# Order of the first score tiles, transposes and squares, and the length of the first run of product halves, in a fused attention and maxout kernel

## The chip, the cores and the metric

The kernel runs on one core of one Trainium2 chip. The metric is device time in microseconds (us) of one execution; lower is better. A profiled execution gives, besides its time, its span from the first to the last instruction.

## The reference

Eight sequences of 3072 tokens go through a gated attention unit without softmax and then through a maxout layer with two input projections.

```python
# u, v: (8, 3072, 256); z: (8, 3072, 64); w1, w2: (256, 1024); w_out: (1024, 256)
scores = (1.0 / S) * np.matmul(z, z.transpose(0, 2, 1))
attn = np.maximum(scores, 0.0) ** 2
out = np.matmul(attn, v)
x = (u * out).reshape(B * S, D)
g = np.maximum(x @ w1, x @ w2)
return g @ w_out
```

## The kernel before

A sequence has 24 blocks of 128 tokens. A step is one window of 512 query tokens (4 blocks), so that there are 6 steps a sequence and 48 in all. Within a step the scores are made in tiles of two key blocks against 512 queries: four matmuls over 64 rows (`score`) write one PSUM pair of 128 x 1024. A relu reads it into SBUF as bf16, on ScalarE or VectorE, and a square follows in place, again on ScalarE or VectorE. The squared tiles multiply v into two accumulators in PSUM. Tiles are named by step and first key block: `("score", 0, 4)` is the third tile of the first step.

Score pairs live in three PSUM slots with the tags w0, w1 and w2 (the pool "mm"). A new tile in a slot waits for the reads of the slot's previous tile. The slots of the first four tiles are fixed as 1, 2, 1, 2; from the fifth tile on, `share_mm` takes for each the slot with the smallest `free_at`, the lower number on a tie.

The first three steps are "plain". In step 0 most products are done as halves: each matmul covers 64 rows of a key block, and the two halves go to the two accumulators. In mode A the first half goes to accumulator 0 and the second to accumulator 1, in mode B the other way round, so each block needs both an A and a B pass. `FIRST_RUNS` lists the runs of step 0 as (mode, first tile, end tile); `put_halves` puts each tile's four A or B matmuls per pair of blocks into the list of work. Between two runs a window of two score tiles is laid in (tiles 8 and 10 after the first run, 12 and 14 after the second, and so on). Where the mode changes, a mark (a nop on GpSimd's queue that waits for TensorE) keeps the two passes apart.

Before that stands the head, which is written out by hand at the end of the function. z is needed transposed (`zT`). The first nine blocks of z of the first sequence come by one DMA, are cast by VectorE and ScalarE, transposed on TensorE and copied to `zT` by VectorE (blocks 0 to 4) and ScalarE (5 to 8). The other blocks come by a second DMA; sixteen transposes write them to `tpz_c`, which takes the tag w0, and VectorE copies them in two parts of eight blocks. `head_pair(k0, part)` issues one part of one score tile of step 0: part 0 the scores, part 1 the relu (VectorE for tile 2, ScalarE for the others), part 2 the square (ScalarE for tile 0, VectorE for the others). The order of these calls is the order on each engine's queue:

```python
    head_pair(0, 0)
    head_pair(2, 0)
    head_pair(0, 1)
    head_pair(2, 1)
    ...  # tpz_c and its sixteen transposes
    head_pair(0, 2)
    ...  # VectorE's two copies
    head_pair(4, 0)
    head_pair(6, 0)
    head_pair(4, 1)
    head_pair(2, 2)
```

Everything else is ordered by a planner inside the kernel's Python. The order of TensorE's work (`pe_order`) follows from the list of work. For the other engines `find_orders` runs a greedy list schedule over assumed durations, which chooses the engine of each relu and square and the order on ScalarE, VectorE, SP (transposing DMAs and stores) and GpSimd's queue (loads). It is run 24 times with changed margins and the order with the earliest end is emitted. The jobs of the head are not planned: they count as done at the time that `HEAD_DONE` gives in nanoseconds, or else as done from the beginning. Wide SBUF tiles get their slots from a first pass of the same schedule (`share_wide`).

Of the kernel before, what the change touches and what calls it, by code (L numbers as in the profile page):

```python
# [11 lines left out]
def kernel(  # L12
# [23 lines left out]
    B, S, D = u.shape  # L36
# [87 lines left out]
    def zT_pe(zT, z_sb, s0, n, tpz=None):  # L124
        flat = z_sb.rearrange("p t d -> p (t d)")
        if tpz is None:
            tpz = mm_psum.tile([P, 8, P], bf16, name="tpz", tag="w0")
        for j in range(n):
            pin(nc.tensor.transpose(tpz[:, j, :], flat[:, ds((s0 + j) * dqk, P)], ident))  # L129
        return lambda copy: pin(copy(zT[:, ds(s0, n), :], tpz[:, :n, :]))  # L130
# [136 lines left out]
    def score(q, out_ps, j, k, s, q0, n):  # L267
        half = ds(j * dqk, dqk)
        matmul(
            out_ps,  # L270
            q.zT[half, k + 1 - j, :],
            q.zT[half, ds(G * s + 1 - j + q0, n), :],
            start=True,
            stop=True,
        )
# [4 lines left out]
    def relu(eng, out_ap, in_ap):  # L280
        if eng == "ACT":
            pin(nc.scalar.activation(out_ap, in_ap, AF.Relu))  # L282
        else:
            pin(nc.vector.tensor_single_scalar(out=out_ap, in_=in_ap, scalar=0.0, op=ALU.max))

    def square(eng, ap):
        if eng == "ACT":
            pin(nc.scalar.activation(ap, ap, AF.Square))  # L288
        else:
            pin(nc.vector.tensor_mul(ap, ap, ap))  # L290
# [21 lines left out]
    def a_tile(st, g):  # L312
        return tile_of(*a_key(st.n, g))
# [3 lines left out]
    def a_half(tile, k0):  # L317
        return tile[:, ds(k0 % G, 2), :].rearrange("p k x -> p (k x)")

    def a_rows(st, k0):  # L320
        return a_half(a_tile(st, k0 // G), k0).rearrange("p (t m x) -> p m t x", t=2, m=2)
# [94 lines left out]
    def s_tile(key):  # L416
        return tile_of("mm", key)

    def by_tokens(s_ps):
        return s_ps.rearrange("p m (t x) -> p m t x", t=2)  # L420
# [910 lines left out]

    turned_order = []
    plain_todo, plain_modes, first_windows = [], {}, []
    FIRST_RUNS = [("A", 0, 1), ("B", 0, 3), ("A", 1, 5), ("B", 3, 6), ("A", 5, 10), ("B", 6, 10)]

    for n, st in enumerate(steps):
        if not st.plain:
# [79 lines left out]
        if n == 0:  # L1417
            for run in FIRST_RUNS:
                first_windows.append(len(work))
# [335 lines left out]
    for pool in ("acc0", "acc1"):  # L1755
# [16 lines left out]
        A=NA, T=NT, es=6, lf=6, xT=LAG, g=2, o=2, e0=1, gs=1, xs=1, u=2, uT=2, mm=1000, acc0=1, acc1=1  # L1772
# [17 lines left out]
    for key, before in zip(pe_order, [None] + pe_order):  # L1790
        if key[0] == "score" and (before is None or plain_modes.get(before) == "F"):
            jobs[key].ways = {"PE": jobs[key].ways["PE"] + 2 * SWITCH}
    HEAD_DONE = {("relu", 0, 4): 900, ("square", 0, 2): 1400}
    HEAD_JOBS = HEAD | {("relu", 0, k0) for k0 in (0, 2, 4)} | {("square", 0, k0) for k0 in (0, 2)}


# [60 lines left out]
    def find_orders():  # L1857
# [14 lines left out]
        def settle(j, begin, ns):  # L1872
            j.begin, j.done = begin, begin + ns + j.lag
            if j.key in FIRST_LOADS:
                j.done = FIRST_LOADS[j.key]
            elif j.dma:

                dma_free[0] = max(dma_free[0], begin + DMA_START["SP" if "SP" in j.ways else "POOL"]) + (DMA_FULL if begin < DMA_FULL_TO else DMA_PART) * j.dma
                j.done = dma_free[0] + (DMA_LATE if begin > 125000 and j.key[0] != "zT" else DMA_END)
                if "SP" in j.ways:  # L1880
                    idle_from["SP"] = max(begin + SP_ISSUE, dma_free[0] - DMA_AHEAD)
            for nxt, _ in j.succ:
                nxt.waits -= 1
                if not nxt.waits:
                    release(nxt)
# [4 lines left out]
        for key in [k for k in jobs if k in HEAD_JOBS]:  # L1890
            settle(jobs[key], HEAD_DONE.get(key, -1), 0)
            for e in jobs[key].ways:
# [59 lines left out]
    def share_mm():  # L1952
        keys = order["mm"]
        uses = [[], [("mm", keys[0]), ("mm", keys[2])], [("mm", keys[1]), ("mm", keys[3])]]
        free_at, last_use = [0, 0, 1], [-1] * 3
        for key, slot in zip(keys, (1, 2, 1, 2)):
            bufs["mm", key].slot = slot
        for key in keys[4:]:
            at = position[taker["mm", key].key]
            slot = min([i for i in range(3) if last_use[i] < at], key=lambda i: free_at[i])  # L1960
            last_use[slot] = max(position.get(j.key, -1) for j in bufs["mm", key].jobs)
            user = pe_order[last_use[slot]]
            reads = 1200
            if key[0] == "o":
                reads = READ_O[0] if steps[key[1]].seven else READ_PLAIN[key[2] % 2]
            free_at[slot] = plan[user] + jobs[user].ways["PE"] + reads
            uses[slot].append(("mm", key))
            bufs["mm", key].slot = slot
        return uses
# [5 lines left out]
    find_orders()  # L1975
    wide = share_wide()
    pairs = share_mm()
    for _ in range(ROUNDS):
        link(wide + pairs)
# [15 lines left out]
    def take(pool, key):  # L1995
        b = bufs[pool, key]
        b.tile = b.make() if b.slot is None else b.make(f"w{b.slot}")

    def head_pair(k0, part):
        key = (0, k0)  # L2000
        if part == 0:
            take("mm", key)
            for j in range(2):
                score(q, s_tile(key)[:, j, :], j, k0 + j, 0, 0, G)
        elif part == 1:
            if k0 % G == 0:
                take("A", (0, k0 // G))
            relu("DVE" if k0 == 2 else "ACT", a_rows(steps[0], k0), by_tokens(s_tile(key)))
        else:
            square("ACT" if k0 == 0 else "DVE", a_half(a_tile(steps[0], k0 // G), k0))  # L2010
# [20 lines left out]
    head_pair(2, 0)  # L2031
    head_pair(0, 1)
    head_pair(2, 1)
    tpz = mm_psum.tile([P, 2, 8, P], bf16, name="tpz_c", tag="w0")
    two = [zT_pe(q.zT, z_sb_0, ZF + 8 * i, 8, tpz[:, i]) for i in range(2)]
    head_pair(0, 2)
    for part in two:
        part(nc.vector.tensor_copy)
    head_pair(4, 0)
    head_pair(6, 0)  # L2040
    head_pair(4, 1)
    head_pair(2, 2)

    taken = set(early_loads)
    for j, e in emitted:
# [35 lines left out]
```

## Time and profile before

| | us |
|---|---|
| timed runs | 885.15, 895.35, 901.41 |
| their median | 895.35 |
| profiled execution, time | 887.8 |
| profiled execution, span | 886.0 |
| TensorE matmuls busy | 877.8 (99%) |
| VectorE busy | 803.3 (91%) |
| ScalarE busy | 753.0 (85%) |
| GpSimd busy | 98.7 (11%) |

The busy times are of the profiled execution, with shares of its span. Matmuls overlap in the array, so that their length in the profile includes the drain of the array; the distance from one start to the next says what one costs. In the profile PE is TensorE, PEld its weight loads, DVE VectorE, ACT ScalarE, POOL GpSimd and SP SyncE. Most operations of an engine share a helper's line (L86 all matmuls but transposes, L129 transposes, L130 the copies into zT, L282 ScalarE's relu, L284 VectorE's relu, L288 ScalarE's square, L290 VectorE's square), so rows are told apart by their tiles.

### The profile page before, as it was taken

To read this page: it belongs to the slowest core of one execution; us is meant where nothing else is said; L and a number is where in the kernel's file an instruction comes from. 1 tells how busy PE (TensorE), PEld (TensorE's weight loads), DVE (VectorE), ACT (ScalarE), POOL (GpSimd) and SP (SyncE) were. 2 spreads that over 40 slices of the span, in tenths; PEclk is the share of its full clock that TensorE was granted. 3 is DMA by queue.
4 is the path that set the end of the run, shared out by engine and by line. 5 is a ranking of instruction groups with operands and counts; after the bars stand their busy time and mean duration, and the time that the engine had idled before them with its cause. 6 is when DMAs were issued, how large, how long until landed. Compare 5 with 4: busy or idle time off the path is not lost.

```text
span 886.0 us, 37887 instructions
## 1 busy us (share of the span) xinstructions
PE 877.8 (99%) x16589; PEld 738.9 (83%) x16589; DVE 803.3 (91%) x1728; ACT 753.0 (85%) x944; POOL 98.7 (11%) x204
## 2 busy tenths in 40 slices
PE   8999999999999999999999999999999999999998
PEld 3468888888888888888888888889888898889886
DVE  6877799989999999989998999989999999999985
ACT  8967998889988999789997899978999799997634
POOL 2100001111011110111101111011100111000000
PEclk9999999999999999999999999999999999999999
DMA  9999999999999989999899998999999999997711
GB/s 159 153 178 165 207 205 185 197 171 146 166 171 189 196 139 152 174 187 188 139 174 171 208 158 144 177 174 182 163 154 172 182 197 147 174 166 134 126 57 73
DMA packets 382085, 146.17 MB, mean 165 GB/s; under 512 B 360416, under 2 KB 362080, under 8 KB 381920
## 3 DMA queue, kind: packets, MB, share of 16 engines
q1 hardware_dynamic: 364128, 114.01, 78.7%
q0 software_dynamic: 17792, 29.75, 24.0%
q8 instruction: 129, 2.11, 1.0%
q14 instruction: 36, 0.29, 0.1%
HBM read 59.77 MB, written 25.17 MB: 96 GB/s over the span
## 4 chain that ended last, share of the span: by engine, by line
PE 96%; ACT 1%; issue 1%; DVE 1%; DMA 1%; POOL 0%; POOLq 0%
PE acc L86 49%; PE s_ps L86 46%; DMA z_sb<-in_z_dram 1%; ACT a_sb L282 0%; ACT a_sb L288 0%; ACT g_last L282 0%; DVE zT L130 0%; DVE o_sb L299 0%; PE tpz_c L129 0%; ACT w2T_sb L293 0%; ACT g_sb L282 0%; PE w2t_ps L1670 0%; DVE o_sb L296 0%; DVE w2T_sb L293 0%; DVE es L296 0%
## 5 line engine op out<-in xcount | busy, mean ns | idle before, releaser
L86 PEld LDWEIGHTS <-v_sb 64*128 64x128 bf16 x4552 | 334.1, 94 | 59.2 <-issue 4.6
L282 ACT ACTIVATE a_sb<-s_ps 128x1024 bf16<-128x1024 f32 (+1 forms) x334 | 302.6, 939 | 32.5 <-PE s_ps L86 28.8
L86 PEld LDWEIGHTS <-lf 64*128 64x128 bf16 x3240 | 264.4, 94 | 15.4 <-POOLq L94 3.2
L86 PE MATMUL acc<-es,v_sb 64*128 64x256 bf16 x2160 | 274.9, 269 | 0.0
L86 PE MATMUL acc<-es,lf 64*128 64x256 bf16 x1080 | 245.1, 269 | 0.0
L86 PE MATMUL acc<-a_sb,lf 64*128 64x256 bf16 x1224 | 232.5, 269 | 0.0
L86 PE MATMUL s_ps<-xT,w_sb 64*128 64x512 bf16 (+1 forms) x1504 | 213.5, 376 | 1.5 <-issue 0.8
L288 ACT ACTIVATE a_sb<-a_sb 128x1024 bf16<-128x1024 bf16 (+1 forms) x217 | 203.8, 965 | 1.5
L282 ACT ACTIVATE g_sb<-s_ps 128x1024 bf16<-128x1024 f32 x187 | 185.8, 1024 | 13.8 <-PE s_ps L86 10.3
L86 PE MATMUL acc<-aT,lf 64*128 64x256 bf16 x936 | 177.9, 269 | 0.0
L86 PE MATMUL acc<-a_sb,v_sb 64*128 64x256 bf16 (+2 forms) x1424 | 141.3, 284 | 0.8 <-issue 0.8
L86 PE MATMUL s_ps<-zT 64*128 64x512 bf16 (+2 forms) x774 | 120.4, 333 | 0.6 <-DVE zT L130 0.6
L86 PEld LDWEIGHTS <-gs 64*128 64x128 bf16 x2816 | 103.0, 94 | 9.6 <-issue 0.6
L296 DVE TENSOR_TENSOR es<-aT 128x1536 bf16<-128x1536 bf16 (+1 forms) x117 | 106.2, 933 | 0.0
L86 PEld LDWEIGHTS <-w_sb 64*128 64x128 bf16 (+1 forms) x1520 | 79.2, 94 | 27.0 <-issue 2.8
L86 PEld LDWEIGHTS <-g_sb 64*128 64x128 bf16 x2304 | 88.0, 94 | 10.4 <-POOLq L94 7.3
L107 POOL DMA_DIRECT2D u_sb<-in_u_dram x89 | 46.1, 518 | 453.1 <-PE acc L86 340.7
L290 DVE TENSOR_TENSOR a_sb<-a_sb 128x1024 bf16<-128x1024 bf16 (+1 forms) x119 | 76.5, 648 | 18.8 <-ACT a_sb L282 17.6
L86 PE MATMUL acc<-aT,v_sb 64*128 64x256 bf16 x936 | 86.9, 269 | 0.0
L299 DVE TENSOR_TENSOR es<-a_sb 128x512 bf16<-128x512 bf16 x198 | 79.3, 422 | 8.2 <-PE acc L86 8.1
L86 PE MATMUL s_ps<-wf_sb,gs 64*128 64x128 bf16 x2112 | 85.0, 216 | 0.0
L296 DVE TENSOR_TENSOR es<-a_sb 128x1024 bf16<-128x1024 bf16 x108 | 72.9, 690 | 0.0
(94 smaller groups left out, 1173.6 us busy)
## 6 DMA issues: line engine op xcount, KB each, us to landing
out_dram<-o_sb SPq DMA_DIRECT2D x47, 512.0 KB, 4.8
u_sb<-in_u_dram POOLq DMA_DIRECT2D x82, 128.0 KB, 4.1
v_sb<-in_v_dram POOLq DMA_DIRECT2D x72, 128.0 KB, 4.6
aT<-a_sb SPq DMA_TRANSPOSE x228, 4.8
v_sb<-in_v_dram POOLq DMA_DIRECT2D x12, 256.0 KB, 6.5
z_sb<-in_z_dram POOLq DMA_DIRECT2D x7, 384.0 KB, 6.6
u_sb<-in_u_dram POOLq DMA_DIRECT2D x7, 256.0 KB, 5.9
w_sb<-in_moe_w_dram POOLq DMA_DIRECT2D x2, 512.0 KB, 7.3
```

The source lines that it names most:

```text
L86: newest[0] = pin(nc.tensor.matmul(*args, **kw)).ins
L107: dma = pin(nc.gpsimd.dma_start(**kw))
L282: pin(nc.scalar.activation(out_ap, in_ap, AF.Relu))
L288: pin(nc.scalar.activation(ap, ap, AF.Square))
L290: pin(nc.vector.tensor_mul(ap, ap, ap))
L296: pin(nc.vector.tensor_add(*args))
L299: pin(nc.vector.tensor_sub(*args))
```

## The change

The scores of the third tile, `head_pair(4, 0)`, are issued ahead of the sixteen transposes of z's second part. VectorE's square of the second tile, `head_pair(2, 2)`, is issued ahead of the two copies out of `tpz_c`. The first run of halves takes tiles 0 and 2 (four blocks) instead of tile 0 alone, and the third run begins with the third tile accordingly. Two settings go with it: the square of tile 2 no longer has a time in `HEAD_DONE`, and the first values of `free_at` make the fifth tile take slot 1 and the sixth slot 0.

```diff
-    FIRST_RUNS = [("A", 0, 1), ("B", 0, 3), ("A", 1, 5), ("B", 3, 6), ("A", 5, 10), ("B", 6, 10)]
+    FIRST_RUNS = [("A", 0, 2), ("B", 0, 3), ("A", 2, 5), ("B", 3, 6), ("A", 5, 10), ("B", 6, 10)]
...
-    HEAD_DONE = {("relu", 0, 4): 900, ("square", 0, 2): 1400}
+    HEAD_DONE = {("relu", 0, 4): 900}
...
-        free_at, last_use = [0, 0, 1], [-1] * 3
+        free_at, last_use = [1, 0, 2], [-1] * 3
...
     head_pair(2, 1)
+    head_pair(4, 0)
     tpz = mm_psum.tile([P, 2, 8, P], bf16, name="tpz_c", tag="w0")
     two = [zT_pe(q.zT, z_sb_0, ZF + 8 * i, 8, tpz[:, i]) for i in range(2)]
     head_pair(0, 2)
+    head_pair(2, 2)
     for part in two:
         part(nc.vector.tensor_copy)
-    head_pair(4, 0)
     head_pair(6, 0)
     head_pair(4, 1)
-    head_pair(2, 2)
```

## The prediction

> **What bounds the kernel now.** I read the page's busy shares first, then the chain that ended last, then a table of stages, and then the head instruction by instruction, because every edited line acts there.
>
> ```profile
> PE 877.8 (99%) x16589; PEld 738.9 (83%) x16589; DVE 803.3 (91%) x1728; ACT 753.0 (85%) x944; POOL 98.7 (11%) x204
> PEclk9999999999999999999999999999999999999999
> PE 96%; ACT 1%; issue 1%; DVE 1%; DMA 1%; POOL 0%; POOLq 0%
> ```
>
> The chain is 96% TensorE at full clock, so time can only come from TensorE standing still. The stages, as busy time per engine in cut-out stretches (length first, then TensorE; the last three columns are granted clock, DMA share and GB/s):
>
> ```profile
> 5.30:8.75 3.45, 2.82 (x29) 1.34 (x30) 2.57 (x4) 3.25 (x5) 0.57 (x2) 1.00 1.08 183
> 8.75:12.64 3.89, 3.89 (x36) 2.00 (x38) 3.31 (x6) 3.89 (x6) 0.40 (x1) 1.00 1.12 205
> 12.64:24.00 11.36, 11.36 (x90) 4.78 (x87) 9.98 (x16) 10.77 (x12) 1.40 (x3) 1.00 1.10 165
> 24.00:175.00 151.00, 150.78 (x2430) 118.37 (x2430) 128.17 (x281) 126.51 (x158) 13.42 (x26) 1.00 1.20 184
> 175.00:200.00 25.00, 23.82 (x445) 20.31 (x441) 21.97 (x46) 21.60 (x28) 4.12 (x8) 1.00 1.23 181
> 200.00:866.00 666.00, 664.99 (x13250) 578.03 (x13247) 626.96 (x1359) 575.74 (x723) 74.13 (x151) 1.00 1.02 163
> 866.00:886.00 20.00, 16.50 (x312) 12.65 (x308) 9.26 (x20) 9.25 (x16) 0.00 (x0) 0.98 0.21 80
> ```
>
> From 8.75 us to 24 us TensorE never pauses; between 24 and 866 us it stands for 0.22 + 1.18 + 1.01 = 2.41 us in all. So the edits are worth exactly the shift of the point from which TensorE runs without a pause, corrected for the work that it has done by then. That point is 8.75 us; the chain of waits says what sets it (start, length, what):
>
> ```profile
> 1.48 4.77 DMA z_sb<-in_z_dram
> ...
> 6.29 1.08 PE tpz_c L129 x16
> 7.38 0.02 issue
> 7.40 1.30 DVE zT L130 x2
> 8.70 0.05 issue
> 8.75 0.60 PE s_ps L86 x4
> ...
> 22.51 2.70 PE acc L86 x12
> ```
>
> The second part of z lands at 6.25, sixteen transposes follow, two VectorE copies, then the scores of tiles 8 and 10 (I call a score tile by its first block, so s8 is ("score", 0, 8)). The head's rows, TensorE, then ScalarE, then VectorE (start, length, instruction):
>
> ```profile
> 5.31 0.61 PE L86 MATMUL s_ps<-zT 64*128 64x512 bf16 x4 [0.36 <-DVE zT L130]
> 6.29 1.07 PE L129 MATMUL tpz_c<-ident,z_sb 128*128 128x128 bf16 x16 [0.38 <-DMA z_sb<-in_z_dram]
> 7.29 0.61 PE L86 MATMUL s_ps<-zT 64*128 64x512 bf16 x4
> 7.91 0.61 PE L86 MATMUL acc<-a_sb,v_sb 64*128 64x512 bf16 x4
> 8.75 0.60 PE L86 MATMUL s_ps<-zT 64*128 64x512 bf16 x4 [0.23 <-DVE zT L130]
> 9.19 1.46 PE L86 MATMUL acc<-a_sb,v_sb 64*128 64x512 bf16 x12
> 10.48 0.59 PE L86 MATMUL s_ps<-zT 64*128 64x512 bf16 x4
> 10.91 1.89 PE L86 MATMUL acc<-a_sb,v_sb 64*128 64x512 bf16 x16
> 12.64 0.59 PE L86 MATMUL s_ps<-zT 64*128 64x512 bf16 x4
> ```
>
> ```profile
> 4.99 0.59 ACT L130 COPY zT<-tpz_b 128x512 bf16<-128x512 bf16 x1 [0.98 <-PE tpz_b L129]
> 5.74 1.02 ACT L282 ACTIVATE a_sb<-s_ps 128x1024 bf16<-128x1024 f32 x1 [0.17 <-PE s_ps L86]
> 6.80 1.06 ACT L288 ACTIVATE a_sb<-a_sb 128x1024 bf16<-128x1024 bf16 x1
> 7.76 5.58 ACT L282 ACTIVATE a_sb<-s_ps 128x1024 bf16<-128x1024 f32 x6
> ```
>
> ```profile
> 4.76 0.49 DVE L130 COPY zT<-tpz 128x640 bf16<-128x640 bf16 x1 [0.83 <-PE tpz L129]
> 5.96 1.22 DVE L284 TENSOR_SCALAR a_sb<-s_ps 128x1024 bf16<-128x1024 f32 x1 [0.70 <-PE s_ps L86]
> 7.40 1.29 DVE L130 COPY zT<-tpz_c 128x1024 bf16<-128x1024 bf16 x2 [0.22 <-PE tpz_c L129]
> 8.61 2.72 DVE L290 TENSOR_TENSOR a_sb<-a_sb 128x1024 bf16<-128x1024 bf16 x4
> ```
>
> The lengths to use are distances between starts, since a matmul's own length includes its drain. Four scores take 10.91 - 10.48 = 0.43, so 0.22 a tile. Twelve products take 10.48 - 9.19 = 1.29, or 0.43 for four. The transposes take 7.29 - 6.29 = 1.00. ScalarE spends 5.58 / 6 = 0.93 on a relu, and from 5.74 on it never stops. A consumer starts about 0.05 us after its producer ends: s8 at 8.75 after copies that end at 8.69, products at 7.91 after the square that ends at 7.86.
>
> Three details decide the sums. First, zT is followed by regions: s0 starts at 5.31, just after VectorE's copy ends at 5.25, though ScalarE's copy into other blocks runs until 5.58. Second, s8 needs only zT's block 9, from the first copy, yet it waits for both, as it takes slot 0, whose last user tpz_c is free only after the second. Third, the first copy starts at 7.40, behind all sixteen transposes (VectorE was free at 7.18, when the first eight were through).
>
> **The change part by part.**
>
> *s4 ahead of the transposes.* No instruction is added or removed. s4 takes slot 1 from tile 0 and so waits for relu 0, which ends at 6.76; it is the head of TensorE's queue, and the sixteen transposes, whose data is there at 6.25, are now queued behind it. s4 runs at 6.82, the transposes from 7.04 instead of 6.29: 0.75 later. They end at 7.04 + 1.07 = 8.11. What s4's earlier start brings to ScalarE is nothing: relu 4 stands behind square 0 there, which ends at 7.86 in either order, and ScalarE is full.
>
> *VectorE's first square ahead of the copies.* Relu 2 ends at 7.18, and VectorE would idle until 8.15. The square of tile 2 (2.72 / 4 = 0.68) fits from 7.18 to 7.86, so it costs nothing: its cover is the wait for the later transposes. Without that cover it would push both copies by 0.68. The copies run from 8.15 to 8.80 and 9.44, against 8.69 before. Square 4 follows at 9.44 instead of 9.30: 0.14 late. Its reader, the last four products of the B run, starts at about 10.59, and the square is through at 10.12, so nothing waits.
>
> *First run of four blocks.* The run A of tiles 0 and 2 has eight products instead of four; the second A run has twelve instead of sixteen. The sum is unchanged, and so are the number of changes between runs and their marks on the POOL queue; each mark keeps a score pair as cover. TensorE: transposes to 8.04, s6 to 8.26 (relu 2 freed slot 2 at 7.18), products of tile 0 to 8.69 (its square was done at 7.86), of tile 2 to 9.12 (square done 7.86).
>
> *Slots.* With free_at [1, 0, 2], s8 goes to slot 1 and s10 to slot 0. s8 waits for relu 4 (7.86 + 0.93 = 8.79) and the first copy (8.80), both past by 9.12, and runs to 9.34. s10 needs the second copy: 9.44 + 0.06 = 9.50. Behind it the B run is queued. TensorE stands for 0.16.
>
> *Sum.* Before, the pauseless stretch begins at 8.75 with s8. After, it begins at 9.50 with s10, while four products (0.43) and s8 (0.22) more are done: 9.50 - 0.43 - 0.22 = 8.85. **Net +0.10 us.** As a cross-check, walking on: B from 9.72, the next scores at 11.01, the A run of twelve from 11.45, the scores after it at 12.74, against 12.64. Relus 6, 8 and 10 would start at 8.79, 9.72 and 10.65, and their scores are there by 8.43, 9.51 and 9.89, so ScalarE keeps its pace. The first timed u load, tied to TensorE's position, moves by the same 0.1.
>
> Bounds. If the first copy can start after eight transposes, it starts at 7.86, both are through by 9.15, s10 follows s8 at 9.34 without a pause, and the sum is 9.34 - 0.65 = 8.69, or -0.06. If the first copy doesn't release s8 alone, s8 starts at 9.50 and the sum is 9.50 - 0.43 = 9.07, or +0.32. I take +0.10, since rows show both behaviours it needs.
>
> *HEAD_DONE and the plan.* The planner now takes square 2 as done from the beginning, where it had set it at 1400 ns. By its costs (432 a pair, 223 a score tile), TensorE waited about 0.3 us inside the first B run, and that wait goes; its clock moves against ScalarE's, VectorE's and the DMA's. Matmul order is fixed by hand and changes only in the head, but which engine takes a relu, the order on VectorE, ScalarE and SP, and the slots of the wide tiles come out of a greedy list with 24 rounds. They may differ anywhere later. The trace can't price that directly. From above, all pauses between 24 and 866 us are 2.41 us, the most that a luckier order can win there; the other side is the last rival.
>
> **Against the medians.** The profiled execution took 887.8 us, with a span of 886.0 and 1.8 around it; the sum gives 887.9. The three timed runs are 885.15, 895.35 and 901.41. Since the same program spreads over 16 us, I carry +0.1 to the mean of these four, 892.4: **892.5 us**. Against their median of 895.35 that is no change; 2% is 18 us, about what a measurement of this kernel can tell from no change.
>
> **The rivals.**
>
> *The new plan is luckier.* The pauses after 24 us go: 887.8 - 2.4 = 885.4. For it: a plan tuned to a false done time is replaced. Against it: 2.4 us is all there is, and the end stretch's 3.5 us belong to the last stores. It can't reach 2%.
>
> *The clock drops.* TensorE now stands from 5.92 to 6.82, 0.90 us against 0.37.
>
> ```profile
> 1.19 2.74 PE L86 MATMUL zeros<-blank 128*128 128x512 bf16 x6 [1.19 <-DVE blank L166]
> 2.44 1.49 PE L86 MATMUL zeros<-blank 128*128 128x512 bf16 x3
> ```
>
> The first matmuls start 0.42 us apart ((2.44 - 1.19) / 3), those at 22.51 follow every 2.70 / 12 = 0.225, although the granted clock reads 1.00 from the start. If the longer pause brought the slow pace back for about the 3.2 us that it lasted at the beginning (1.19 to some 4.4, my estimate from the transposes' shortening), 1.5 us would be lost: 889.4. Against it: the pause of 0.37 and others of under 1 us here did nothing. The Trainium skill, "TensorE: Matmul & The Clock Gate", section "Part 1: The HAM clock gate", has this as a rule: half rate returns only after an idle window of about 3.4 us. By it 0.90 us is too short, and the sum stays +0.10.
>
> *Slower: the new order makes transposes late.* Between 24 and 200 us the DMA share is 1.20 and more, so one transfer put ahead of another delays it by its whole time.
>
> ```profile
> aT<-a_sb SPq DMA_TRANSPOSE x48, 5.5
> ```
>
> A turned tile lands 5.5 us after issue in this stretch (median). If SP's new order puts one transfer ahead of a turned tile that step 3 or later reads, TensorE waits up to 5.5 us at that step's Xa products; everything behind is in order. One such place gives 893.4 on the profiled execution, five give 915.3, over 2%; it decides from about four. For it: DMA is full there, and the spread of 16 us of an unchanged program is what such lateness could make. Against it: in the trace TensorE's waits from 24 to 200 us come to 1.4 us, so the slack at each reader is not near zero.
>
> **How the numbers follow.** Forecast 0.72; luckier plan 0.10; clock 0.03; late transposes 0.15, of which 0.12 beyond 2%, as a whole order is at stake rather than one tile. Faster by over 2% would need less than the 877.8 us of TensorE work, so only timing noise gives it 0.02. The range: below, the luckiest run, 885.15, less a little, 884.5; above, the slowest run with one late transpose, 901.41 + 5.5 = 906.9, 907.
>
> **What would show it.** Right: s4 about 6.82, the transposes about 7.04, a VectorE square between relu 2 and the copies, s8 about 9.1, s10 about 9.5, the scores after the second A run near 12.74, TensorE busy near 877 us, and pauses from 24 to 866 us within a few us. Wrong: s4 starting with s2, copies before 8.1, s10 without a pause, slow matmuls after 6.8 us, or pauses of several us at Xa products in the DMA-full stretch.

## The result: 0.4% slower, and the profile after

| | median us | lowest to highest | executions | above 891 us |
|---|---|---|---|---|
| before | 888.69 | 885.15 to 901.41 | 22 | 7 |
| after | 894.26 | 885.58 to 898.08 | 22 | 16 |

The ratio after to before is 1.004, 95% interval 1.0021 to 1.0059: 3.5 us slower by the ratio. That is within 2%, but it isn't nothing. The lowest times agree (885.15 and 885.58). What changed is how often an execution lies in the upper group.

The profiled execution of after does not show the loss: it took 887.82 us with a span of 886.0, and before took 887.8 with 886.0. Its page has the same busy times, but another chain: TensorE's share has gone from 96% to 90%, and VectorE's from 1% to 5%.

```profile
PE 877.3 (99%) x16589; PEld 739.4 (83%) x16589; DVE 803.8 (91%) x1729; ACT 751.2 (85%) x943; POOL 98.7 (11%) x204
PE 90%; DVE 5%; DMA 2%; issue 1%; ACT 1%; SPq 0%; POOL 0%; ACTq 0%; DVEq 0%; POOLq 0%
```

**The head** came out close to the sum. First TensorE of after (start, length, instruction, idle time before it), then VectorE. A score tile is two matmuls, not four as the section on the kernel before has it: s4 alone is the row at 6.70 with x2, and a row with x4 holds two tiles.

```profile
5.20 0.60 PE L86 MATMUL s_ps<-zT 64*128 64x512 bf16 x4 [0.36 <-DVE zT L130]
6.70 0.39 PE L86 MATMUL s_ps<-zT 64*128 64x512 bf16 x2 [0.90 <-ACT a_sb L282]
7.03 1.07 PE L129 MATMUL tpz_c<-ident,z_sb 128*128 128x128 bf16 x16
...
9.12 0.75 PE L86 MATMUL s_ps<-zT 64*128 64x512 bf16 x4
9.71 1.46 PE L86 MATMUL acc<-a_sb,v_sb 64*128 64x512 bf16 x12
...
12.73 0.60 PE L86 MATMUL s_ps<-zT 64*128 64x512 bf16 x4
```

```profile
7.10 0.69 DVE L290 TENSOR_TENSOR a_sb<-a_sb 128x1024 bf16<-128x1024 bf16 x1
8.13 1.29 DVE L130 COPY zT<-tpz_c 128x1024 bf16<-128x1024 bf16 x2 [0.34 <-PE tpz_c L129]
```

VectorE's square now fills the wait for the transposes. The scores after the A run start at 12.73; the same work of before started at 12.64. So between these two executions the head costs 0.09 us.

**Behind the head.** The stages of after (length, then busy time of TensorE, its weight loads, VectorE, ScalarE and GpSimd; the last three columns are granted clock, DMA share and GB/s):

```profile
12.75:24.00 11.25, 11.25 (x89) 4.73 (x86) 9.48 (x15) 10.59 (x12) 1.26 (x2) 1.00 1.12 173
24.00:175.00 151.00, 149.40 (x2386) 117.57 (x2386) 127.82 (x280) 124.03 (x155) 13.43 (x26) 1.00 1.23 176
175.00:200.00 25.00, 25.00 (x488) 21.64 (x486) 23.41 (x50) 22.46 (x31) 4.12 (x8) 1.00 1.26 181
200.00:866.00 666.00, 665.19 (x13253) 578.43 (x13250) 626.94 (x1359) 575.68 (x723) 74.14 (x151) 1.00 1.03 164
```

TensorE stands for 1.60 us between 24 and 175 us (0.22 before), not at all up to 200 us (1.18 before), and 0.81 us up to 866 us (1.01 before). The sum is 2.41 us, as before, but the pause sits elsewhere and has another releaser. ScalarE, then TensorE of after near 148 us:

```profile
147.83 1.94 ACT L282 ACTIVATE a_sb<-s_ps 128x1024 bf16<-128x1024 f32 x2 [2.20 <-DMA aT<-a_sb]
```

```profile
148.91 0.40 PE L86 MATMUL s_ps<-w_out_sb,g_sb 64*128 64x128 bf16 x8 [1.50 <-ACT a_sb L282]
```

A relu on ScalarE waits 2.20 us for a transposing DMA, the last reader of the wide SBUF slot that the relu writes; TensorE waits 1.50 us for the PSUM tile that this relu frees. This wait isn't in before's trace.

**The plan moved.** Set side by side, the two emitted orders show that TensorE's differs in the head alone, while those of the other engines differ in several places up to step 9, and then only in VectorE's order of a few sums of steps 45 and 46. Three squares of step 8 change between ScalarE and VectorE, VectorE's list differs from its 12th planned job on, and one load changes places with its neighbour. Two wide slots exchange their whole contents, which leaves the order of tiles in each as it was. On SP's queue the transpose of u of step 4 (uT 4) goes eight places later, behind seven other transposes and a store. The traces show it, before first (SP's own queue; start, length, instruction):

```profile
77.10 1.25 SPq L103 DMA_TRANSPOSE uT<-u_sb  x1
95.41 1.27 SPq L103 DMA_TRANSPOSE uT<-u_sb  x1
```

```profile
52.03 3.33 SPq L103 DMA_TRANSPOSE uT<-u_sb  x1
95.15 2.71 SPq L103 DMA_TRANSPOSE uT<-u_sb  x2
```

What before issues at 77.10 after issues at 95.15, together with the next one. The load of u of step 6, which reuses the buffer that uT 4 reads, follows later too, at 100.02 instead of 97.00.

### The profile page after: what moved, and what is told of

Its sections match the earlier page's. It is cut to its first block, busy times and chain, and to the rows that moved or that the text cites. A ratio compares the mean times of both kernels' runs of the same rounds, so it can differ in the third digit from the quotient of the medians.

```text
span 886.0 us, 37888 instructions
## 1 busy us (share of the span) xinstructions
PE 877.3 (99%) x16589; PEld 739.4 (83%) x16589; DVE 803.8 (91%) x1729; ACT 751.2 (85%) x943; POOL 98.7 (11%) x204
## 4 chain that ended last, share of the span: by engine, by line
PE 90%; DVE 5%; DMA 2%; issue 1%; ACT 1%; SPq 0%; POOL 0%; ACTq 0%; DVEq 0%; POOLq 0%
PE acc L86 46%; PE s_ps L86 43%; DVE es L296 1%; DVE es L299 1%; DVE a_sb L299 1%; DMA v_sb<-in_v_dram 1%; DMA aT<-a_sb 1%; DMA uT<-u_sb 0%; DVE gs L299 0%; DVE o_sb L299 0%; ACT a_sb L282 0%; DVE xT L303 0%; ACT g_sb L282 0%; DMA o_sb<-in_z_dram 0%; DVE o_sb L296 0%
## 5 line engine op out<-in xcount | busy, mean ns | idle before, releaser
L86 PE MATMUL s_ps<-w_out_sb,g_sb 64*128 64x128 bf16 (+1 forms) x1600 | 72.8, 222 | 1.5 <-ACT a_sb L282 1.5
```

Of the source, the lines that this page charges most:

```text
L86: newest[0] = pin(nc.tensor.matmul(*args, **kw)).ins
```

## The experiments

Each variant carries a recorded order for some engines. `TAKEN` names the engines whose order, with the wide slots, comes from the other kernel's plan; `MOVE` puts one job right behind another on its queue; `PLACES` holds a load back until that many jobs of TensorE are out. No work is added or removed. Each ran 12 times. The variants ran in four groups (e0 to e3, e5 to e8, e10 to e13, e14 to e16), each with its own executions of before beside it, on chips 7, 5, 5 and 1. A fold, in the names below, is a sum on VectorE over blocks of v, and a turn is the transposing DMA of one tile of squared scores. The last column counts executions whose mean granted clock was 0.998 or less, which one interval at half clock is enough to make (below).

| variant | base | ratio to before, 95% | above 891 us | low clock |
|---|---|---|---|---|
| e0 | after, unchanged | 1.0027 [1.0001, 1.0054] | 8 of 12 | 6 of 12 |
| e1 | after's head, before's plan | 1.0004 [0.9975, 1.0033] | 4 | 5 |
| e2 | before's head, after's plan | 1.0042 [1.0008, 1.0076] | 10 | 8 |
| e3 | after, SP of before | 1.0028 [1.0000, 1.0056] | 7 | 4 |
| e5 | after, uT 4 and loads of before | 1.0008 [0.9972, 1.0043] | 5 | 6 |
| e6 | before, loads of after | 1.0004 [0.9978, 1.0029] | 4 | 1 |
| e7 | before, loads and uT 4 late | 1.0046 [1.0016, 1.0075] | 9 | 11 |
| e8 | before, u of step 6 early | 1.0001 [0.9970, 1.0032] | 6 | 7 |
| e10 | after, uT 4 alone of before | 1.0015 [0.9973, 1.0056] | 6 | 7 |
| e11 | before, fold later | 0.9992 [0.9956, 1.0028] | 5 | 4 |
| e12 | after, fold later | 1.0003 [0.9967, 1.0040] | 6 | 2 |
| e13 | before, fold later, turn earlier | 0.9956 [0.9924, 0.9989] | 0 | 0 |
| e14 | before, turn earlier | 0.9991 [0.9961, 1.0021] | 3 | 3 |
| e15 | after, turn earlier | 1.0040 [1.0007, 1.0073] | 10 | 10 |
| e16 | after, both | 0.9995 [0.9960, 1.0029] | 4 | 1 |

Executions of before above 891 us: 7 of 35 beside e0 to e3, 14 of 35 beside e5 to e8, 16 of 34 beside e10 to e13, 9 of 29 beside e14 to e16; of low clock 8, 14, 15 and 10. They differ between the groups, so ratios are compared, and a count only beside that of before in its group.

### Head or plan

e0 is after once more. e1 and e2 take the change apart:

```diff
 # e1: after's FIRST_RUNS, free_at and head_pair order
+TAKEN = ('ACT', 'DVE', 'SP', 'POOL')   # from before's plan
 # e2: before's FIRST_RUNS, free_at and head_pair order
+TAKEN = ('ACT', 'DVE', 'SP', 'POOL')   # from after's plan
```

> The changed kernel once more, unaltered, for another profile and more times. Both theories: a ratio near 1.004 to before, with executions in two groups, about 887 us and about 895 us. Theory PLAN (the other engines' new order makes a DMA transpose late, a relu waits for its slot, TensorE waits for the relu): in an execution of the upper group TensorE's missing time lies near 148 us, 2 to 6 us of it, with ScalarE's relu released by a DMA aT<-a_sb. Theory HEAD (the 0.9 us pause in front of the third score tile lets the clock fall): the time is lost before 15 us, with matmuls 0.42 us apart instead of 0.22 for some 3 us.

> The changed head and first runs (TensorE's order and its PSUM slots as after the change), but the order on ScalarE, VectorE, SP and GpSimd's queue and the wide SBUF slots as in the kernel before. PLAN: ratio 1.000 to before, within 0.2%; relu (8, 20) not held by a DMA near 147 us. HEAD: ratio 1.004, as the full change.

> The kernel before with its own head and TensorE order, but the order on ScalarE, VectorE, SP and GpSimd's queue and the wide SBUF slots as after the change. PLAN: ratio 1.004, and the wait of a relu for aT<-a_sb near 147 us. HEAD: ratio 1.000.

The new head with the old plan can't be told from before (1.0004); the old head with the new plan has a loss as large as the whole one (1.0042). So the plan makes after slower by itself, and no loss is seen from the head. The interval of e1 reaches 1.0033, so a smaller share of the head is not excluded. The wait of a relu near 147 us that was expected for e2 is not in its profile. That shows another wait, which after's own profile had not (TensorE, then VectorE):

```profile
116.64 0.39 PE L86 MATMUL acc<-a_sb,v_sb 64*128 64x256 bf16 x4 [2.76 <-DVE e L296]
```

```profile
115.83 0.42 DVE L296 TENSOR_TENSOR lf<-v_sb 128x512 bf16<-128x512 bf16 x1 [2.74 <-DMA v_sb<-in_v_dram]
```

VectorE's fold of v waits 2.74 us for a load of v. The sum into `e` that frees TensorE's accumulator stands behind it in VectorE's queue, and TensorE waits 2.76 us for that. The releaser named in TensorE's row is the last operation before it; the cause is one row further, in VectorE's. In after's profile the same fold had its load in time, at 112.59, so this wait comes in some executions only.

### Which part of the plan

e3 gives after the SP order of before; e5 puts only uT 4 and two loads back to before's places, e10 only uT 4; e6 gives before the later loads, e7 the later uT 4 as well, and e8 an earlier load of u.

```diff
 # e3 (after)
+TAKEN = ('SP',)
 # e5 (after)
+PLACES = {('u', 6): 193, ('v', 1, 5): 202}
+MOVE = [('SP', ('uT', 4), ('turn', 1, 22))]
 # e10 (after; the loads where after has them)
+PLACES = {('u', 6): 201, ('v', 1, 5): 204}
+MOVE = [('SP', ('uT', 4), ('turn', 1, 22))]
 # e6 (before)
+PLACES = {('u', 6): 201, ('v', 1, 5): 204}
 # e7 (before): as e6, and
+MOVE = [('SP', ('uT', 4), ('turn', 4, 22))]
 # e8 (before)
+PLACES = {('u', 6): 178}
```

> The changed kernel with only SP's order (transposes and stores) put back to that of before; ScalarE's and VectorE's order and the wide slots stay as after the change. PLAN with SP's order as the cause (uT of step 4 seven places later, uT of step 6 one place later): ratio 1.000 and no wait near 147 us. PLAN with ScalarE's and VectorE's order as the cause (squares of step 8 on other engines): ratio 1.004. HEAD: ratio 1.004.

> The changed kernel with one thing of the plan put back as before: the transposing DMA uT of step 4 at its old place in SP's queue (seven places earlier), and the loads of u of step 6 and of v's group 5 at their old places against TensorE. Everything else as after the change. Theory LOAD (uT 4 late, so its u buffer is late, so the load of u 6 starts at 100 instead of 97 us, on top of the v loads at 100.7 and 104.8, which then land late): ratio 1.000 to before, load of u at 97 us, no TensorE wait over 1 us between 100 and 160 us. Theory ORDER (the new order on VectorE and ScalarE is the cause): ratio 1.003 to 1.004, waits near 115 or 150 us as in the full change.

> The changed kernel with only uT of step 4 back at its old place in SP's queue; the loads of u of step 6 and v's group 5 stay where the change has them. Theory TRANSPOSE (uT 4 at 94 us instead of 77 lies in the crowded stretch just ahead of the v loads and makes them land late): ratio 1.000 to 1.001, as with the loads put back too. Theory LOAD (the load's time counts): 1.003 to 1.004.

> The kernel before, with only the loads of u of step 6 and v's group 5 moved to where the changed kernel has them against TensorE (about 3 us and 0.6 us later). LOAD: ratio 1.003 to 1.004, v's fold on VectorE waits for its DMA near 113 us. ORDER: ratio 1.000.

> As e6_u6_late, and uT of step 4 at its late place in SP's queue too. LOAD: ratio 1.003 to 1.004. ORDER: ratio 1.000. If it is slower than e6_u6_late, the place of the transpose counts by itself beside the load.

> The kernel before, with only the load of u of step 6 moved earlier, some 5 us ahead of its place at 97 us, so that it lies between the v loads instead of in front of one. LOAD: not slower than before, ratio 0.997 to 1.000, and fewer executions above 891 us. ORDER: 1.000.

Two answers are plain. The later loads by themselves cost nothing (e6, 1.0004), nor does an earlier one (e8, 1.0001). SP's order by itself does not bring before's time back (e3, 1.0028): its profile has both waits, 1.28 us at 115.10 and 1.57 us at 151.45. The rest isn't plain. e5 and e10 lie between before and after (1.0008 and 1.0015), with intervals that hold both. e7 is slow (1.0046), as a late uT 4 should make it, but by a wait of its own: before's VectorE order wants uT 4 at about 93 us, and there its operation stood still.

```profile
97.81 0.69 DVE L303 SCALAR_TENSOR_TENSOR xT<-e,uT 128x512 bf16<-128x512 f32 x1 [4.21 <-DMA uT<-u_sb]
```

So which single difference of the order makes v land late stays open. The traces show that v's loads take longer with after's plan: the two loads of v issued from 95 to 118 us have a median from issue to landing of 4.9 to 6.5 us in the seven traces with before's plan and uT 4 early (before, e1, e6, e8, e11, e13, e14), and of 6.6 to 10.0 us in the nine made from after's plan. They speak against uT 4 as the only cause: with it back at its early place the loads still take 10.0 us (e3), 8.0 (e5) and 6.7 (e10). e3 has the whole SP order of before, so the order on VectorE and ScalarE, with the one exchanged load, is the rival that is left; no run put that back alone. The rows of these loads, with the median last, in before, in after and in e15:

```profile
v_sb<-in_v_dram POOLq DMA_DIRECT2D x2, 256.0 KB, 6.5
```

```profile
v_sb<-in_v_dram POOLq DMA_DIRECT2D x2, 256.0 KB, 7.0
```

```profile
v_sb<-in_v_dram POOLq DMA_DIRECT2D x2, 256.0 KB, 9.7
```

### The two waits

Over all traces the two waits go with the plan. In each of the seven made from after's plan with the fold left in its place (after, e0, e2, e3, e5, e10, e15) TensorE stands 1.01 us or more at one of the two places, and in none of the seven with before's plan named above (three of which have a reader moved).

The next variants leave the transfers late and take away who waits for them. The fold goes behind the sum that frees the accumulator; the transpose of step 7's tile 10, on whose slot the relu near 148 us waits, goes earlier on SP.

```diff
 # e11 (before), e12 (after)
+MOVE = [('DVE', ('fold', 1, 2, 0), ('ye', 5))]
 # e14 (before), e15 (after)
+MOVE = [('SP', ('turn', 7, 10), ('turn', 6, 22))]
 # e13 (before), e16 (after)
+MOVE = [('DVE', ('fold', 1, 2, 0), ('ye', 5)), ('SP', ('turn', 7, 10), ('turn', 6, 22))]
```

> The kernel before, with one sum on VectorE, the first fold of v's last pair of sequence 1 (lf<-v_sb), moved two places later, behind the sums that free TensorE's accumulators. If late v loads are what makes an execution of before slow at times (the fold blocks VectorE, and TensorE waits for an accumulator): fewer executions above 891 us than before, ratio 0.997 to 0.999. If the upper group has other causes: 1.000.

> The changed kernel with the same fold behind the same sum (one place later). If the wait near 115 us is the larger part of the loss: ratio to before 1.001 to 1.002. If the wait of a relu near 150 us is the larger part: 1.003 to 1.004 still.

> The kernel before, with only the transpose of tile 10 of step 7 four places earlier in SP's queue. Theory SLOT (an execution is slow when relu (8, 20) waits for this transpose, and TensorE for the relu): ratio near 0.996 and no execution above 891 us, as in e13_fold_turn. Theory BOTH (the late fold counts as much): about 0.998, with some above 891 us.

> The changed kernel with only this transpose four places earlier. SLOT: ratio to before 0.996 to 0.998, the change's loss gone. BOTH: about 1.001, with TensorE waits near 115 us left in the slow executions.

> As e11_fold_later, and the transpose of tile 10 of step 7, for which relu (8, 20) waits as its slot's last reader, four places earlier in SP's queue. Both waits are eased: ratio 0.996 to 0.999 if they are what is left, 1.000 otherwise.

> The changed kernel with this transpose four places earlier and the fold behind the next sum on VectorE. Both theories: the loss of the change gone, ratio 0.995 to 0.998, the same as e13_fold_turn within 0.2%. If another consequence of the new order is at work, such as uT of step 4 delaying other transfers: 1.001 or more.

In after, moving the fold brings the ratio to 1.0003, with low clocks in 2 of 12 executions, beside 15 of 34 of before in its group. Moving the turn alone leaves 1.0040, and 10 of 12, beside 10 of 29. This points to the fold's wait as the larger part and to the slot's wait, the one that after's profile shows, as the smaller; I had expected e15 to gain. It isn't shown: the intervals of e12 and e15 overlap between 1.0007 and 1.0040, and e12's holds the whole loss of 1.004. e15's profile shows the whole chain. VectorE's rows, then the chain of waits from 104 to 122 us (start, length, what):

```profile
112.25 0.42 DVE L299 TENSOR_TENSOR e<-acc,e 128x256 f32<-128x256 f32 x1
115.98 0.43 DVE L296 TENSOR_TENSOR lf<-v_sb 128x512 bf16<-128x512 bf16 x1 [3.31 <-DMA v_sb<-in_v_dram]
116.33 0.41 DVE L296 TENSOR_TENSOR e<-e,acc 128x256 f32<-128x256 f32 x1
```

```profile
104.90 10.99 DMA v_sb<-in_v_dram
115.89 0.03 issue
115.92 0.02 DVEq L296
115.94 0.04 issue
115.98 0.43 DVE lf L296
116.41 0.34 DVE e L296
116.75 0.04 issue
116.79 1.99 PE acc L86 x18
```

One load of v takes 10.99 us, the fold waits 3.31 us for it, the sum into `e` comes next, and 0.04 us after it TensorE goes on, having stood for 3.34 us. Not all of e15's loss is this one: its profile has two more pauses, of 1.66 and 2.31 us near 521 and 595 us, with no releaser named.

```profile
594.93 0.39 PE L86 MATMUL acc<-a_sb,v_sb 64*128 64x256 bf16 x1 [2.31 <-issue]
```

e5's profile, of 893.58 us, has its longest pause there too, 3.07 us at 519 us. The two plans order this stretch alike, and a pause of 1.11 us at 519 us is also in e8, which has before's plan. So some of the executions above 891 us lose time where the change of plan reorders nothing, and the cause of that is open.

In before the fold alone (e11) and the turn alone (e14) bring nothing that can be told from 1, but together they do: **e13 takes 0.9956 of before's time** (887.89 us against 890.78), none of its 12 executions is above 891 us, and its highest is 890.92. Its interval ends at 0.9989, and it overlaps those of e11 and e14, so that both moves are needed is not shown. after did not run beside e13; its own ratios are 1.0040 and 1.0027. The stages of e13:

```profile
24.00:175.00 151.00, 150.85 (x2424) 118.34 (x2424) 128.16 (x280) 126.81 (x158) 13.47 (x26) 1.00 1.15 176
175.00:200.00 25.00, 25.00 (x477) 21.74 (x472) 23.38 (x50) 22.74 (x30) 4.66 (x9) 1.00 1.24 207
200.00:866.00 666.00, 665.52 (x13262) 577.53 (x13259) 627.13 (x1358) 575.83 (x723) 73.88 (x150) 1.00 1.04 164
```

TensorE stands for 0.15 us up to 200 us and 0.48 us up to 866. With after's plan the same two moves reach 0.9995 (e16): no wait near 115 or 150 us reaches 1 us, but another of 1.69 us appears near 136 us, where the scores wait for a relu.

```profile
135.87 0.39 PE L86 MATMUL s_ps<-zT 64*128 64x512 bf16 x2 [1.69 <-ACT g_sb L282]
```

## Why the prediction failed, step by step

**The head's sum held, with some luck.** Every edited operation ran within 0.12 us of its forecast time (s4 at 6.70 for 6.82, transposes 7.03 for 7.04, copies 8.13 for 8.15, B run 9.71 for 9.72). s0, and s4 with it, started 0.11 us earlier in this execution, but from s4 to the transposes took 0.33 us where the sum has 0.22, and the two offsets cancel. The net was +0.09 us for +0.10. A tenth can't be read from one pair of traces: the scores after the second A run start from 12.72 to 13.20 us in eight of the nine traces with the new head, and from 12.64 to 13.14 in the eight with the old. VectorE's first square cost nothing, under the cover named.

**The clock rival was not empty.** In after the matmuls did not slow down behind the pause of 0.90 us. In e12, the ninth trace with the new head, they are slow ahead of the pause (the first four scores take 1.04 us, against 0.60 in after) and stay so behind it:

```profile
7.09 0.61 PE L86 MATMUL s_ps<-zT 64*128 64x512 bf16 x2 [0.69 <-ACT a_sb L282]
7.63 1.89 PE L129 MATMUL tpz_c<-ident,z_sb 128*128 128x128 bf16 x16
9.45 0.61 PE L86 MATMUL s_ps<-zT 64*128 64x512 bf16 x2
```

Its sixteen transposes take 9.45 - 7.63 = 1.82 us, against 1.00 in after, and the scores after the second A run start at 14.52, at least 1.3 us behind the other eight, with a granted clock of 1.00 in these rows. That is near the rival's price of 1.5 us. One trace does not show how often this happens, or whether the old head has it too.

**The step that failed is "HEAD_DONE and the plan".** It stood in the forecast at nothing, with a bound of 2.41 us on the gain and its loss left to a rival with a chance of 0.15. What the runs showed in its place: the new order alone costs 1.0042 (e2), about 3.7 us, and in its trace TensorE stands 2.76 us for a late load of v, a wait that before's trace has not. The rival's argument against itself, that slack at each reader isn't near zero as TensorE waits only 1.4 us from 24 to 200 us, was drawn from one undisturbed execution. The same two loads of v take 7.0 us (median) in after's trace and 8.7 us in e0's, the same kernel, so one trace can't show their slack.

**The rival "the new order makes transposes late" had the direction, but another reader.** Its place was the Xa products of turned tiles, at 5.5 us each. The runs showed two others: a relu that takes a slot whose last reader is a late transpose (1.50 us here, 2.20 us in e0), and a fold of v on VectorE with the freeing of an accumulator queued behind it (2.76 us in e2, 3.34 us in e15). Pauses of 2.20 us and more also brought a slow clock that cost 1.7 us or more, which the rival did not count. Which difference of the order makes the loads late stays open.

**The level was off as well.** 892.5 was 0.1 more than the mean of four executions of before. With 22, before's median is 888.69, so that the level was too high by about 3.7 us, and the change's cost too low by about as much. That 892.5 lies near 894.26 is luck: the two errors offset each other.

**The sign named for a wrong forecast was blind.** Pauses from 24 to 866 us "within a few us" held, 2.41 for 2.41, and TensorE's busy time was 877.3 as forecast, in an execution of the lower group.

**The luckier plan** did not come. Its bound, 2.41 us, is too small for what a median can win: e13 gains 0.44%, some 3.9 us. That other executions of before have pauses that its profiled one hasn't would explain it, but no slower execution of before was traced.

## What to carry to other kernels

A constant that feeds a planner is an edit of the whole kernel: compare the emitted queues of every engine, or freeze the order of the others, before an edit is priced at its own place. In a queue that runs in order, put no operation that waits for a DMA ahead of the one that frees PSUM for TensorE; where the DMA's time varies from execution to execution, one profile without the wait proves no slack. Moving two such operations, with no work changed, won 0.44% here (e13), more than the 0.10 us that the edit of the head was forecast to cost.

## What the hardware showed that I had not expected

A pause of TensorE costs more than itself from a certain length. These are one-us windows of e15 behind its pause of 3.34 us, which ends at 116.79; granted clock, DMA share and GB/s come last:

```profile
116.00:117.00 1.00, 0.21 (x4) 0.21 (x5) 1.00 (x3) 0.00 (x0) 0.00 (x0) 0.97 1.19 437
117.00:118.00 1.00, 1.00 (x14) 0.84 (x11) 1.00 (x4) 0.00 (x0) 0.20 (x1) 0.50 1.05 302
118.00:119.00 1.00, 1.00 (x11) 0.66 (x9) 1.00 (x4) 0.00 (x0) 0.32 (x1) 0.50 1.28 287
119.00:120.00 1.00, 1.00 (x12) 0.87 (x10) 1.00 (x3) 0.76 (x1) 0.00 (x0) 0.50 1.11 180
120.00:121.00 1.00, 1.00 (x20) 0.83 (x17) 1.00 (x4) 0.53 (x2) 0.00 (x0) 0.82 1.56 174
121.00:122.00 1.00, 1.00 (x44) 1.00 (x40) 1.00 (x4) 1.00 (x2) 0.00 (x0) 1.00 0.91 193
```

The clock is at half for about 3.4 us, and the missing shares add up to 0.03 + 3 x 0.50 + 0.18 = 1.71 us. In e0 it is the same behind a pause of 2.20 us:

```profile
152.73 0.56 PE L86 MATMUL s_ps<-w_out_sb,g_sb 64*128 64x128 bf16 x8 [2.20 <-ACT a_sb L282]
```

```profile
152.00:153.00 1.00, 0.27 (x8) 0.27 (x9) 0.29 (x1) 1.00 (x2) 0.00 (x0) 0.91 1.08 201
153.00:154.00 1.00, 1.00 (x24) 1.00 (x21) 1.00 (x4) 0.97 (x2) 0.00 (x0) 0.50 1.07 207
...
156.00:157.00 1.00, 1.00 (x24) 0.80 (x21) 0.00 (x0) 0.31 (x1) 0.00 (x0) 0.88 0.94 206
```

The same 1.71 us is missing behind the pauses of 2.31 us (e15), 2.76 (e2) and 3.07 (e5). e7 lost more: its clock fell during a pause of 3.23 us and stayed at half until about 113.4 us, some 7 us in all, with 3.41 us missing. After pauses of 1.50 us (after), 1.57 (e3), 1.66 (e15) and 1.69 (e16) the clock stayed at full. So by an estimate from these rows a wait of 2.2 us costs about 3.9 us or more, and one of 1.7 us costs 1.7. One interval of 1.71 us is 0.002 of 886 us, and of after's 16 executions above 891 us, 15 have a mean clock of 0.998 or less. Part of the two groups of times is this step; how much of the 3.5 us it makes was not separated.

The Trainium skill, "TensorE: Matmul & The Clock Gate", section "Part 1: The HAM clock gate (the "warmup" mystery)", puts the return to half rate behind an idle window of about 3.4 us, and the return to full rate behind a busy window of the same length. The second agrees with the slow stretch of about 3.4 us measured in e15 and e0. The first does not agree with the pauses, since 2.20 us was enough here and 1.69 us was not.
